# wi2 packed early into the vacated half of xT, low halves on VectorE, and each tile's maximum first: one edit to an attention + two-FFN kernel on Trainium2

## The chip, the cores and the metric

One core of one Trainium2 chip runs the whole program. The metric is device time in microseconds (us), the median of several executions. Engines: TensorE (PE for matmuls, PEld for weight loads), VectorE (DVE), ScalarE (ACT), GpSimd (POOL) and SyncE (SP, which here issues the loads).

## The reference

Three stages, all in float32:

```python
# attention: 2 batches x 8 heads, 576 tokens, head size 64, rotary q and k
attn = softmax(q_rot @ k_rot.T / 8);  x = attn @ v         # -> x: 1152 tokens x 512
# gated FFN, 512 -> 1536 -> 512
x2 = ((x @ w_a) * (x @ w_b)) @ w_out
# SoLU FFN, 512 -> 1024 -> 512
h = x2 @ w_in
solu = h * softmax(h)                                      # over the 1024 columns
ln = (solu - mean) / sqrt(var + 1e-6) * g_ln               # over the 1024 columns
out = ln @ w_out2
```

The FFN weights of this program arrive as 64-bit floats. The kernel reads them as pairs of 32-bit integers and puts float32 values together from them on the chip ("packing").

## The kernel before, in words

Every float32 matmul is done as three products of a high half and a low half (high x high, high x low, low x high). So each operand has two parts: the high half is a cast on ScalarE, the low half is the operand minus its high half, on VectorE or GpSimd.

**Weights.** 36 pieces of weights are numbered in the order of their use: 0 to 11 are w_a and w_b, 12 to 19 are w_out ("x", 768 columns each), 20 to 27 are wi2, the reference's second w_in ("h", 512 columns each), 28 to 35 are wo2 ("out", 512 columns each). For each piece, `load_n` allocates its place and lets SyncE issue the load into a raw buffer; `pack` builds float32 in a second buffer `f` in five steps (step 0 an absolute value on ScalarE, L87; steps 1 to 4 on VectorE, L89, L91, L93, L95); `split` makes the high half on ScalarE (`high`, L101, for "out" pieces behind a scaling, L100) and the low half (`low`, L104) on GpSimd, or on the engine that is passed. There are two raw and two `f` buffers, used in turn; from piece 20 on a buffer is two halves of 512 columns. `load_after(n)` issues the next loads once the last step of pack n stands in the queue, since the raw buffer is free from then on.

**Buffers that are used twice.** The three products of a, b and x are kept in `gT` tiles by token block t (0, 1, 2, of 384 tokens each). The split weights of wi2 go where `gT` of t = 0 was, those of wo2 where t = 1 was, and the rows `et` of the last stage where t = 2 was (the first one elsewhere). So wi2 can be split only when the last x2 block of t = 0 is done. `xT` (128 x 4 x 2 x 1152) holds x transposed, high and low, for the w_a/w_b matmuls (L580), and then x2 transposed.

**The x2 stage** (L705 to L729): 12 blocks (m, t) of 36 matmuls (L711), in the order (0,0) (0,1) (0,2) (1,0) (1,1) (1,2) (2,0) (3,0) (2,1) (3,1) (2,2) (3,2). Blocks with even m take turns in two PSUM buffers, those with odd m in two others. `x2_out` copies a block to `xT` on ScalarE (L718) and subtracts on VectorE (L719). Beside each block stand steps of the weights, by the dictionary `beside`.

**The last stage**, for nine tiles of 128 tokens: `hmm` (h, L744, 24 matmuls; two PSUM buffers in turn), `chain1` (the maximum on VectorE, L756; the exponential with its sum on ScalarE, L757), `chain2` (the sum's reciprocal, L762 and L763; the product that reads h in PSUM for the last time, L764; mean and variance, L767 to L770; a power on GpSimd, L772), `chain3` (L777), `ltp` (transposes on TensorE, L786; copy, L789; subtraction, L790), `out_half` (12 matmuls, L815) and `store`. h 0 to h 2 are mixed with the end of x2; from then on a loop runs h i+3, the first output half of tile i, `chain1` of i+3, `ltp` of i+1, the second output half of i, `chain2`, `store` and `chain3`.

The order on every engine is the order of the calls: nothing is rescheduled, and each engine works its queue in order. Waits follow from data and buffers.

Of the kernel before, what the change touches and what calls it, by code (L numbers as in the profile page):

```python
# [12 lines left out]
F32R = mybir.dt.float32r  # L13
I32 = mybir.dt.int32
AF = mybir.ActivationFunctionType
ALU = mybir.AluOpType
# [4 lines left out]
B, H, S, D = 2, 8, 576, 64  # L21
NT, DM, DF1, DF2 = B * S, 512, 1536, 1024
P = 128
NP = H // 2
# [4 lines left out]
CW = 384  # L29
# [40 lines left out]
def _raw(ap):  # L70
    return ap.bitcast(F32)
# [36 lines left out]
def attention_gated_ffn_solu_ffn(ctx: ExitStack, tc, q, k, v, wa, wb, wo1, wi2, wo2, gln, rope_cs, out):  # L108

    nc = tc.nc  # L110
    const = ctx.enter_context(tc.tile_pool(name="const", bufs=1))
# [6 lines left out]
    ident = const.tile([P, P], F32, name="ident")  # L118
    g_sb = const.tile([P, DF2 // P], F32, name="g_sb")
    mhalf = const.tile([P, 1], F32, name="mhalf")  # L120
    xT = const.tile([P, NP, 2, NT], F32R, name="xT")

# [2 lines left out]
    W, wt = {}, {}  # L127
# [7 lines left out]
    def load_w(key, w, raw, t):  # L135
        kind, n = key
        scale = None
        if kind == "ab":
            rv = raw.rearrange("p (m k c) t -> p m k (c t)", m=2, k=4)
            for m, src in enumerate((wa, wb)):  # L140
                nc.sync.dma_start(
                    out=rv[:, m], in_=src[:, 2 * n * P:2 * (n + 1) * P].rearrange("(k p) c -> p k c", p=P)
                )
        elif kind == "x":
            m, half = divmod(n, 2)
            raw, t = raw[:, :6 * P], t[:, :6 * P]
            nc.sync.dma_start(
                out=raw.rearrange("p (f c) t -> p f (c t)", f=6),
                in_=wo1[half * 6 * P:(half + 1) * 6 * P, 2 * m * P:2 * (m + 1) * P].rearrange("(f p) c -> p f c", p=P),
            )  # L150
        else:
            half = slice(n % 2 * DM, (n % 2 + 1) * DM)
            raw, t, w = raw[:, half], t[:, half], w[:, :, half]
            if kind == "h":
                src = wi2[n // 2 * P:(n // 2 + 1) * P, n % 2 * 2 * DM:(n % 2 + 1) * 2 * DM]
            else:
                src, scale = wo2[n * P:(n + 1) * P, :], g_sb[:, n:n + 1]
            nc.sync.dma_start(out=raw.rearrange("p c t -> p (c t)"), in_=src)
        W[key] = Weights(nc, raw, t, w, scale)
# [302 lines left out]

    def x_cols(u):
        b, pr = divmod(u, NP)
        return xT[:, pr, :, b * S:(b + 1) * S]

    def x_mult(u):
        if HI["x"] == "pool":
            nc.gpsimd.tensor_tensor(x_cols(u)[:, 0], x0[u], rb[u], op=ALU.mult)
        nc.gpsimd.tensor_tensor(x0[u], x0[u], rb.pop(u), op=ALU.mult)  # L470

    def x_hi(u):
        if HI["x"] != "pool":
            copy(HI["x"], x_cols(u)[:, 0], x0[u])

    def x_lo(u):
        dst = x_cols(u)
        nc.gpsimd.tensor_tensor(dst[:, 1], x0.pop(u), _raw(dst[:, 0]), op=ALU.subtract)
# [93 lines left out]
    gT, pab = {}, {}  # L572

    def ab_some(f, t, m, ks):
        if (f, t) not in pab:
            pab[f, t] = ps_s.tile([P, 2, 512], F32, tag="s", name=f"ab{f}_{t}")
        wf = W["ab", f].w.rearrange("p a (m k c) -> p a m k c", m=2, k=4)
        for kk in ks:
            for a, xa in ((0, 0), (0, 1), (1, 0)):
                nc.tensor.matmul(  # L580
                    pab[f, t][:, m, :CW], wf[:, a, m, kk, :], xT[:, kk, xa, t * CW:(t + 1) * CW],
                    start=(kk == a == xa == 0), stop=(kk == 3 and a == 1),
                )

# [15 lines left out]
    for f, loaded, steps in ((0, 54.0, W_POS[:6]), (1, W_POS[4] + 0.1, W_POS[6:])):  # L600
        key = ("ab", f)
        add(loaded, lambda key: load_w(key, wtile(w0, "w", key), raw0, f0), key)
        for i, pos in enumerate(steps[:5]):
            add(pos, lambda key, i: W[key].pack((i,)), key, i)
        for pos in steps[5:]:
            add(pos, lambda key: W[key].high(), key)
            add(pos + 1, lambda key: W[key].low(nc.gpsimd), key)
    for i, pos in enumerate(AB):
        add(pos, ab_some, 0, 0, i // 4, (i % 4,))
# [10 lines left out]
    NW, NX = len(order), NF + 8  # L620
    raw1, f1 = buffers(wp)

    def load_n(n):
        key = order[n]
        if n < NX:
            w = wtile((w0, wp)[n % 4 // 2], "w", key)
            odd = n % 2
        else:
            kind, half = key
            if half % 2 == 0:  # L630
                wt[kind, half // 2] = wtile(gpool, f"g{int(kind == 'out')}{half // 2}", key)
            w = wt[kind, half // 2]
            odd = half // 2 % 2
        load_w(key, w, *((raw1, f1), (raw0, f0))[odd])

    def load_after(n):

        ahead = (3,) if n == 1 else (n + 2,) if n < NX - 2 else (2 * n - NX + 4, 2 * n - NX + 5) if n < NX else (n + 4,)
        for m in ahead:
            if m < NW:  # L640
                load_n(m)

    def pack(n, steps=range(5)):
        W[order[n]].pack(steps)
        if 4 in steps:
            load_after(n)
# [24 lines left out]
    for i, (f, t) in enumerate(groups):  # L671
# [5 lines left out]
        for fn, *args in parts[ends[i - 1] if i else 0:ends[i]]:  # L677
            fn(*args)


    x2T = xT
    rest, dve = (1, 2, 3, 4), nc.vector
    beside = {
        (0, 0): [(pack, 15), (split, 15)],
        (0, 1): [(pack, 16)],
        (0, 2): [(pack, 17)],
        (1, 0): [(split, 16), (split, 17)],
        (1, 1): [(pack, 18)],
        (1, 2): [(pack, 19)],
        (2, 0): [(split, 18, dve), (split, 19, dve), (pack, 20), (pack, 21)],  # L690
        (3, 0): [(pack, 22), (pack, 23)],
        (2, 1): [
            (split, 20, dve), (split, 21), (pack, 24, (0,)), (split, 22), (pack, 24, rest), (pack, 25, (0,)), (split, 23),
            (pack, 25, rest),
        ],
        (3, 1): [
            (pack, 26), (split, 24), (pack, 27), (split, 25), (pack, 28, (0,)), (pack, 29, (0,)),
            (pack, 28, rest),
        ],
        (2, 2): [  # L700
            (split, 26), (split, 27), (pack, 29, rest), (pack, 30), (pack, 31, (0,)), (split, 28), (split, 29), (pack, 31, rest),
        ],
    }

    def x2_mm(m, t):  # L705
        pool, tag = ((ps_t, "t"), (ps_o, "o"))[m % 2]
        px[m, t] = o = pool.tile([P, 512], F32, tag=tag, name=f"x2_{m}_{t}")
        for f in range(NF):
            wx = W["x", 2 * m + f // 6].w[:, :, f % 6 * P:(f % 6 + 1) * P]
            for a, ga in ((0, 0), (0, 1), (1, 0)):  # L710
                nc.tensor.matmul(  # L711
                    o[:, :CW], wx[:, a], gT[f // 3, t][:, f % 3, ga], start=(f == 0 and a == ga),
                    stop=(f == NF - 1 and a == 1),
                )

    def x2_out(m, t):
        o, c0 = px.pop((m, t)), t * CW
        nc.scalar.copy(x2T[:, m, 0, c0:c0 + CW], o[:, :CW])  # L718
        nc.vector.tensor_tensor(  # L719
            x2T[:, m, 1, c0:c0 + CW], o[:, :CW], _raw(x2T[:, m, 0, c0:c0 + CW]), op=ALU.subtract  # L720
        )

    px = {}
    order_x2 = [(m, t) for m in (0, 1) for t in range(3)] + [(m, t) for t in range(3) for m in (2, 3)]
    for m, t in order_x2[:-2]:
        x2_mm(m, t)
        for fn, *args in beside[m, t]:
            fn(*args)
        x2_out(m, t)  # L729


    NK2 = DF2 // P
# [3 lines left out]
    def hmm(i):  # L736
        s = ps_s.tile([P, 2, 512], F32, tag="s", name=f"h{i}")
        ph[i] = s
        c0 = i * P
        idx = 0  # L740
        for kk in range(4):
            for xa, a in ((0, 0), (0, 1), (1, 0)):
                for c in range(2):
                    nc.tensor.matmul(  # L744
                        s[:, c], x2T[:, kk, xa, c0:c0 + P], wt["h", kk][:, a, c * 512:(c + 1) * 512],
                        start=(idx == 0), stop=(idx == 11),
                    )
                idx += 1
# [76 lines left out]

    for fn, *args in (
        (x2_mm, 2, 2), *beside[2, 2], (hmm, 0), (x2_out, 2, 2),
        (x2_mm, 3, 2), (pack, 32, (0,)), (split, 30), (chain1, 0), (pack, 33, (0,)), (pack, 32, rest), (split, 31),  # L830
        (chain2, 0), (hmm, 1), (x2_out, 3, 2), (pack, 34, (0,)), (chain3, 0), (pack, 33, rest), (split, 32),
        (chain1, 1), (hmm, 2), (pack, 35, (0,)), (pack, 34, rest), (split, 33), (chain2, 1), (ltp, 0), (split, 34),
        (chain3, 1), (pack, 35, rest), (chain1, 2), (split, 35), (chain2, 2), (chain3, 2),
    ):
        fn(*args)
    for i in range(NTT):
        j = i + 3
        if j < NTT:
# [49 lines left out]
```

## Time and profile before

| what | value |
|---|---|
| median of 3 runs (lowest to highest) | 521.57 us (521.37 to 522.39) |
| the profiled execution, its own time | 522.98 us |
| its span, first to last instruction | 520.1 us |
| mean granted TensorE clock over the span | 0.984 of full speed |
| busy: PE / PEld / DVE / ACT / POOL | 492.8 / 463.7 / 383.9 / 270.0 / 178.3 us |

Times in rows are counted from the start of the span. A row of a time line gives the start, the busy time, the engine, the source line, the operation and what it writes and reads; in brackets stands how long the engine was idle before it and who released it. x followed by a number counts instructions merged into the row. The granted clock is given as a share of full speed (2.4 GHz).

### The profile page before, as it was taken

To read this page: it belongs to the slowest core of one execution; us is meant where nothing else is said; L and a number is where in the kernel's file an instruction comes from. 1 tells how busy PE (TensorE), PEld (TensorE's weight loads), DVE (VectorE), ACT (ScalarE), POOL (GpSimd) and SP (SyncE) were. 2 spreads that over 40 slices of the span, in tenths; PEclk is the share of its full clock that TensorE was granted. 3 is DMA by queue.
4 is the path that set the end of the run, shared out by engine and by line. 5 is a ranking of instruction groups with operands and counts; after the bars stand their busy time and mean duration, and the time that the engine had idled before them with its cause. 6 is when DMAs were issued, how large, how long until landed. Compare 5 with 4: busy or idle time off the path is not lost.

```text
span 520.1 us, 7992 instructions
## 1 busy us (share of the span) xinstructions
PE 492.8 (95%) x2992; PEld 463.7 (89%) x2992; DVE 383.9 (74%) x595; ACT 270.0 (52%) x562; POOL 178.3 (34%) x128
## 2 busy tenths in 40 slices
PE   4889999999989999999999999999999969999997
PEld 4779988989888999999999999999999848888886
DVE  5899999999999767666756755645899996755450
ACT  2699998998898444343444333332354433222221
POOL 5598988788135003111122311220054321000000
PEclk9699999999999999999999999999999979999999
DMA  5334223225002143222332111334434200000011
GB/s 142 85 94 104 70 72 95 73 70 153 25 13 93 45 151 129 82 81 82 102 110 93 62 62 60 122 121 136 172 101 161 81 0 21 20 22 20 21 40 40
DMA packets 50914, 41.97 MB, mean 81 GB/s; under 512 B 23765, under 2 KB 46868, under 8 KB 50876
## 3 DMA queue, kind: packets, MB, share of 16 engines
q1 hardware_dynamic: 50124, 40.48, 26.0%
q10 hardware_dynamic: 624, 0.82, 0.5%
q8 instruction: 23, 0.38, 0.3%
q0 software_dynamic: 128, 0.17, 0.2%
q14 instruction: 15, 0.12, 0.1%
HBM read 37.00 MB, written 2.39 MB: 76 GB/s over the span
## 4 chain that ended last, share of the span: by engine, by line
PE 69%; DVE 15%; ACT 7%; DMA 4%; issue 2%; SPq 1%; POOL 1%; POOLq 0%; DVEq 0%; ACTq 0%
PE ab L580 29%; PE x L711 10%; PE out L815 10%; PE h L744 7%; PE pv L405 4%; PE s L327 4%; ACT e L344 2%; PE t L356 2%; DVE f L95 2%; DVE f L93 2%; DMA qd<-in_q_dram 2%; DVE nm L336 2%; DVE f L91 1%; PE lt L786 1%; ACT pT L370 1%
## 5 line engine op out<-in xcount | busy, mean ns | idle before, releaser
L580 PE MATMUL ab<-xT,wab 128*128 128x384 f32 x864 | 151.9, 336 | 0.0
L580 PEld LDWEIGHTS ab<-xT,wab 128*128 128x128 f32 x864 | 150.7, 188 | 0.1
L711 PE MATMUL x<-gT,wx 128*128 128x384 f32 x432 | 75.9, 336 | 0.0
L711 PEld LDWEIGHTS x<-gT,wx 128*128 128x128 f32 x432 | 75.6, 188 | 0.1
L104 POOL TENSOR_TENSOR wab<-f,wab 128x1024 fp32r<-128x1024 f32 x11 | 26.4, 2398 | 119.2 <-ACT wab L101 103.2
L327 PE MATMUL s<-kS,qS 128*128 128x288 f32 x320 | 60.1, 316 | 1.2 <-ACT e L344 1.2
L744 PE MATMUL h<-wh,xT 128*128 128x512 f32 x216 | 54.4, 409 | 5.1 <-DVE et L764 5.1
L344 ACT ACTIVATE e<-s,nm 128x576 f32<-128x576 f32 x72 | 53.5, 743 | 5.7 <-DVE nm L336 5.0
L744 PEld LDWEIGHTS h<-wh,xT 128*128 128x128 f32 x216 | 42.4, 197 | 15.5 <-issue 5.0
L336 DVE TENSOR_REDUCE nm<-s 128x1 f32<-128x576 f32 x72 | 53.7, 746 | 2.2 <-PE s L327 1.2
L815 PE MATMUL out<-wout,lnT 128*128 128x512 f32 (+1 forms) x240 | 52.9, 373 | 0.0
L374 DVE TENSOR_TENSOR pT<-t,pT 128x512 fp32r<-128x512 f32 x72 | 49.4, 686 | 3.2 <-ACT pT L370 2.2
L327 PEld LDWEIGHTS s<-kS,qS 128*128 128x128 f32 x320 | 47.2, 195 | 4.2 <-ACT e L344 3.4
L815 PEld LDWEIGHTS out<-wout,lnT 128*128 128x128 f32 x240 | 41.4, 188 | 7.5
L405 PE MATMUL pv<-pT,V 128*128 128x288 f32 x288 | 46.0, 304 | 0.8 <-DVE pT L392 0.5
L356 PE MATMUL t<-ident,e 128*128 128x128 f32 x288 | 43.9, 275 | 0.1
L370 ACT CAST pT<-t 128x512 fp32r<-128x512 f32 x72 | 42.3, 587 | 1.1 <-PE t L356 0.5
L405 PEld LDWEIGHTS pv<-pT,V 128*128 128x128 f32 x288 | 39.3, 188 | 2.0 <-POOL V L251 0.8
L588 ACT COPY a<-ab 128x384 f32<-128x384 f32 x36 | 17.3, 479 | 45.4 <-PE ab L580 44.7
L597 DVE TENSOR_TENSOR gT<-a,gT 128x384 fp32r<-128x384 f32 x36 | 23.1, 641 | 21.8 <-ACT gT L596 21.8
L89 DVE TENSOR_SCALAR f<-f 128x512 f32<-128x512 f32 (+2 forms) x36 | 28.7, 797 | 12.5 <-ACT f L87 12.5
L757 ACT ACTIVATE et<-h,mx 128x1024 f32<-128x1024 f32 x9 | 10.0, 1116 | 52.1 <-DVE mx L756 52.1
(132 smaller groups left out, 712.2 us busy)
## 6 DMA issues: line engine op xcount, KB each, us to landing
raw<-in_moe_w_a_dram SPq DMA_DIRECT2D x12, 512.0 KB
raw<-in_moe_w_b_dram SPq DMA_DIRECT2D x12, 512.0 KB
raw<-in_moe_w_out_dram SPq DMA_DIRECT2D x8, 768.0 KB
raw<-in_moe_w_in_dram SPq DMA_DIRECT2D x8, 512.0 KB
raw<-in_moe_w_out_dram SPq DMA_DIRECT2D x8, 512.0 KB
kraw<-in_k_dram SPq DMA_DIRECT2D x16, 128.0 KB
vraw<-in_v_dram SPq DMA_DIRECT2D x8, 256.0 KB
qd<-qd SPq DMA_DIRECT2D x7, 288.0 KB
```

Of the source, the lines that this page charges most:

```text
L89: eng.tensor_scalar(_raw(t), _raw(t), LOW_END, HIGH_END, op0=ALU.max, op1=ALU.min)
L327: nc.tensor.matmul(s[:, c, :KC], qS[u % 2][:, a, off:off + P], kS[u % 2][:, h, c * KC:(c + 1) * KC], start=(m == 0), stop=(m == last),)
L336: nc.vector.tensor_reduce(t, ps[n][:, :, :KC], axis=AX.XY, op=ALU.max, negate=True)
L344: nc.scalar.activation(t.rearrange("p (c n) -> p c n", c=2), ps.pop(n)[:, :, :KC], AF.Exp, bias=nm.pop(n), accum_out=sums[u][:, i:i + 1],)
L356: nc.tensor.transpose(t[:, j, :], e[n][:, j * P:(j + 1) * P], ident)
L370: nc.scalar.copy(hi, src)
L374: nc.vector.tensor_tensor(lo, src, _raw(hi), op=ALU.subtract)
L405: nc.tensor.matmul(o[:, :KC], w[:, h, 4 if m == 8 else m % 4].rearrange("p a d -> p (a d)"), t[:, m, c * KC:(c + 1) * KC], start=(m == 0), ...
L580: nc.tensor.matmul(pab[f, t][:, m, :CW], wf[:, a, m, kk, :], xT[:, kk, xa, t * CW:(t + 1) * CW], start=(kk == a == xa == 0), stop=(kk == 3 ...
L711: nc.tensor.matmul(o[:, :CW], wx[:, a], gT[f // 3, t][:, f % 3, ga], start=(f == 0 and a == ga), stop=(f == NF - 1 and a == 1),)
L744: nc.tensor.matmul(s[:, c], x2T[:, kk, xa, c0:c0 + P], wt["h", kk][:, a, c * 512:(c + 1) * 512], start=(idx == 0), stop=(idx == 11),)
L815: nc.tensor.matmul(o[:, cols], t[:, la, kk, :], w[:, a, cols], start=(kk == la == a == 0), stop=(kk == NK2 - 1 and la == 1),)
```

## The change

- `xT` becomes four tiles, one for each m. The tiles of m = 2 and 3, which x2 needs late, are given up after the w_a/w_b stage: two staging tiles take their place, and pieces 20 to 27 are packed there and not in `f`. x2 of m = 2 and 3 is allocated there again when its first block is written (in `x2_out`), once the staged pieces are split.
- The loads follow a new table: pieces 20 to 23 are loaded behind packs 16 and 17, ahead of 18 and 19.
- Packs 20 to 23 move into blocks (1,0) and (1,1), pack 18 into (1,2), pack 19 into (2,0), packs 24 to 27 into (2,0) and (3,0). Splits 20 to 27 stand together in block (2,1), ahead of the outputs of (2,0) and (3,0).
- All low halves from piece 15 on are made on VectorE.
- In the last list, `chain1` of a tile stands ahead of steps of the packs, and these stand between `chain1` and `chain2`.

```diff
@@ -118,7 +118,8 @@
-    xT = const.tile([P, NP, 2, NT], F32R, name="xT")
+    xp = ctx.enter_context(tc.tile_pool(name="xp", bufs=1))
+    xT = [xp.tile([P, 2, NT], F32R, tag=f"x{m}", name=f"xT{m}") for m in range(NP)]
@@ -152,6 +153,7 @@
             if kind == "h":
+                t = staged[n // 4][:, n % 4]
                 src = wi2[n // 2 * P:(n // 2 + 1) * P, n % 2 * 2 * DM:(n % 2 + 1) * 2 * DM]
...
@@ -633,10 +635,11 @@
+    waiting = {1: (3,), 16: (20, 21), 17: (22, 23), 20: (), 21: (18,), 22: (), 23: (19,), 18: (24, 25), 19: (26, 27)}
+
     def load_after(n):
-
-        ahead = (3,) if n == 1 else (n + 2,) if n < NX - 2 else (2 * n - NX + 4, 2 * n - NX + 5) if n < NX else (n + 4,)
-        for m in ahead:
+        for m in waiting.get(n, (n + 2 if n < 16 else n + 4,)):
             if m < NW:
                 load_n(m)
@@ -678,29 +681,11 @@
-    x2T = xT
+    x2T = list(xT)
+    staged = [xp.tile([P, 4, DM], I32, tag=f"x{m}", name=f"staged{m}") for m in (2, 3)]
     rest, dve = (1, 2, 3, 4), nc.vector
-    beside = {
-        (0, 0): [(pack, 15), (split, 15)],
-        (0, 1): [(pack, 16)],
-        (0, 2): [(pack, 17)],
-        (1, 0): [(split, 16), (split, 17)],
-        (1, 1): [(pack, 18)],
-        (1, 2): [(pack, 19)],
-        (2, 0): [(split, 18, dve), (split, 19, dve), (pack, 20), (pack, 21)],
-        (3, 0): [(pack, 22), (pack, 23)],
-        (2, 1): [
-            (split, 20, dve), (split, 21), (pack, 24, (0,)), (split, 22), (pack, 24, rest), (pack, 25, (0,)), (split, 23),
-            (pack, 25, rest),
-        ],
...
     def x2_out(m, t):
+        if m > 1 and t == 0:
+            x2T[m] = xp.tile([P, 2, NT], F32R, tag=f"x{m}", name=f"x2T{m}")
         o, c0 = px.pop((m, t)), t * CW
-        nc.scalar.copy(x2T[:, m, 0, c0:c0 + CW], o[:, :CW])
+        nc.scalar.copy(x2T[m][:, 0, c0:c0 + CW], o[:, :CW])
...
-    for m, t in order_x2[:-2]:
-        x2_mm(m, t)
-        for fn, *args in beside[m, t]:
-            fn(*args)
-        x2_out(m, t)
+    run(
+        (x2_mm, 0, 0), (pack, 15), (split, 15, dve), (x2_out, 0, 0),
+        (x2_mm, 0, 1), (pack, 16), (x2_out, 0, 1),
+        (x2_mm, 0, 2), (pack, 17), (x2_out, 0, 2),
+        (x2_mm, 1, 0), (split, 16, dve), (split, 17, dve), (pack, 20), (pack, 21), (x2_out, 1, 0),
+        (x2_mm, 1, 1), (pack, 22), (pack, 23), (x2_out, 1, 1),
+        (x2_mm, 1, 2), (pack, 18), (x2_out, 1, 2),
+        (x2_mm, 2, 0), (split, 18, dve), (pack, 19), (split, 19, dve), (pack, 24),
+        (x2_mm, 3, 0), (pack, 25), (pack, 26), (pack, 27),
+        (x2_mm, 2, 1), (split, 20, dve), (split, 21, dve), (split, 22, dve), (split, 23, dve), (x2_out, 2, 0),
+        (split, 24, dve), (split, 25, dve), (split, 26, dve), (split, 27, dve), (x2_out, 3, 0),
+        (x2_out, 2, 1),
+        (x2_mm, 3, 1), (pack, 28), (pack, 29), (pack, 30), (x2_out, 3, 1),
+    )
@@ -825,14 +824,14 @@
-    for fn, *args in (
-        (x2_mm, 2, 2), *beside[2, 2], (hmm, 0), (x2_out, 2, 2),
-        (x2_mm, 3, 2), (pack, 32, (0,)), (split, 30), (chain1, 0), (pack, 33, (0,)), (pack, 32, rest), (split, 31),
-        (chain2, 0), (hmm, 1), (x2_out, 3, 2), (pack, 34, (0,)), (chain3, 0), (pack, 33, rest), (split, 32),
-        (chain1, 1), (hmm, 2), (pack, 35, (0,)), (pack, 34, rest), (split, 33), (chain2, 1), (ltp, 0), (split, 34),
-        (chain3, 1), (pack, 35, rest), (chain1, 2), (split, 35), (chain2, 2), (chain3, 2),
-    ):
-        fn(*args)
+    run(
+        (x2_mm, 2, 2), (split, 28, dve), (split, 29, dve), (pack, 31), (pack, 32, (0,)), (split, 30, dve), (hmm, 0),
+        (x2_out, 2, 2), (split, 31, dve), (pack, 32, (1, 2)), (x2_mm, 3, 2), (pack, 33, (0,)), (chain1, 0),
+        (pack, 32, (3, 4)), (chain2, 0), (hmm, 1), (pack, 34, (0,)), (chain3, 0), (pack, 33, rest), (split, 32, dve),
+        (x2_out, 3, 2), (pack, 35, (0,)), (chain1, 1), (hmm, 2), (pack, 34, rest), (split, 33, dve), (chain2, 1),
+        (ltp, 0), (chain3, 1), (split, 34, dve), (pack, 35, (1, 2)), (chain1, 2), (pack, 35, (3, 4)), (chain2, 2),
+        (split, 35, dve), (chain3, 2),
+    )
```

The matmuls index `xT[m]` and `x2T[m]` in place of `xT[:, m]`; `run` calls a list of steps in order.

## Rows read from the trace of the kernel before

**Rows 1.** Busy time by stretch; columns as in the first line.

```profile
core 0: us, PE busy (x) PEld busy (x) DVE busy (x) ACT busy (x) POOL busy (x), PEclk, DMA share, GB/s
324.40:362.80 38.40, 38.40 (x221) 38.40 (x220) 21.40 (x28) 11.03 (x18) 7.36 (x4) 1.00 0.36 118
...
393.65:423.00 29.35, 24.27 (x117) 20.52 (x117) 28.13 (x43) 14.62 (x26) 8.90 (x8) 0.98 0.28 88
423.01:431.33 8.32, 8.32 (x25) 6.62 (x26) 7.25 (x12) 2.15 (x4) 2.24 (x3) 0.67 0.00 0
437.76:443.35 5.59, 5.59 (x26) 4.53 (x25) 3.74 (x8) 2.65 (x5) 0.00 (x0) 1.00 0.13 47
```

**Rows 2.** Time line of TensorE: h 1, h 2 and h 3.

```profile
405.50 5.74 PE L744 MATMUL h<-wh,xT 128*128 128x512 f32 x24
411.58 5.81 PE L744 MATMUL h<-wh,xT 128*128 128x512 f32 x24 [0.34 <-DVE et L764]
...
423.01 8.32 PE L744 MATMUL h<-wh,xT 128*128 128x512 f32 x24 [4.75 <-DVE et L764]
```

**Rows 3.** The chain that ended last: start, time, what (an output half, the transposes).

```profile
431.33 2.78 PE out L815 x12
434.11 0.87 PE lt L786 x8
```

**Rows 4.** Time line of all engines: a low half on GpSimd and a pack's step.

```profile
385.92 1.29 POOL L104 TENSOR_TENSOR wh<-f,wh 128x512 fp32r<-128x512 f32 x1 [1.28 <-PE x L711]
386.02 1.48 DVE L91 TENSOR_SCALAR f<-f 128x512 int32<-128x512 int32 x1
```

**Rows 5.** Groups by line, VectorE, 376.4 to 431 us: count, busy, mean ns, idle before.

```profile
L95 DVE SCALAR_TENSOR_TENSOR f<-raw,f 128x512 int32<-128x512 int32 x12 | 11.4, 951 | 0.4
L93 DVE SCALAR_TENSOR_TENSOR f<-raw,f 128x512 int32<-128x512 int32 x12 | 11.3, 941 | 0.4
```

**Rows 6.** The same view, VectorE, 364 to 376.4 us, GpSimd idle.

```profile
L93 DVE SCALAR_TENSOR_TENSOR f<-raw,f 128x512 int32<-128x512 int32 x4 | 2.8, 692 | 0.1
...
L104 DVE TENSOR_TENSOR wh<-f,wh 128x512 fp32r<-128x512 f32 x1 | 0.7, 692 | 0.0
```

**Rows 7.** Time line of VectorE: lows 18 and 19, pack 20, later a subtraction and maximum 0.

```profile
363.62 1.83 DVE L104 TENSOR_TENSOR wx<-f,wx 128x768 fp32r<-128x768 f32 x2 [0.23 <-ACT wx L101]
365.37 0.42 DVE L89 TENSOR_SCALAR f<-f 128x512 f32<-128x512 f32 x1
...
367.01 0.69 DVE L95 SCALAR_TENSOR_TENSOR f<-raw,f 128x512 int32<-128x512 int32 x1
367.62 0.42 DVE L89 TENSOR_SCALAR f<-f 128x512 f32<-128x512 f32 x1
...
405.85 0.55 DVE L719 TENSOR_TENSOR xT<-x,xT 128x384 fp32r<-128x384 f32 x1
406.32 1.21 DVE L756 TENSOR_REDUCE mx<-h 128x1 f32<-128x1024 f32 x1
```

**Rows 8.** Time lines of SyncE's queue and ScalarE: a 512 KB load, and its first reader.

```profile
385.25 0.33 SPq L158 DMA_DIRECT2D raw<-in_moe_w_out_dram  x1
...
388.77 0.68 ACT L87 ACTIVATE f<-raw 128x512 f32<-128x512 f32 x1 [2.35 <-DMA raw<-in_moe_w_out_dram]
```

**Rows 9.** Groups by line, ScalarE, 393.65 to 431 us.

```profile
L100 ACT ACTIVATE f<-f,g_sb 128x512 f32<-128x512 f32 x7 | 5.0, 717 | 2.4 <-DVE f L95 2.4
L101 ACT CAST wout<-f 128x512 fp32r<-128x512 f32 x7 | 4.3, 620 | 0.2
L757 ACT ACTIVATE et<-h,mx 128x1024 f32<-128x1024 f32 x3 | 3.3, 1116 | 16.0 <-DVE mx L756 16.0
...
L757 ACT ACTIVATION_READ_ACCUMULATOR et<-h,mx 128x1 f32 x2 | 0.4, 193 | 0.0
```

**Rows 10.** Time line of VectorE in a later tile: `chain2` and `chain3`.

```profile
449.79 0.15 DVE L762 TENSOR_SCALAR sm<-sm 128x1 f32<-128x1 f32 x1
...
450.17 1.28 DVE L764 SCALAR_TENSOR_TENSOR et<-et,sm,h 128x1024 f32<-128x1024 f32 x1
...
453.93 0.81 DVE L777 TENSOR_SCALAR et<-et,mv,rs 128x1024 f32<-128x1024 f32 x1 [0.73 <-POOL rs L772]
```

More of the change, by code (lines that the diff above doesn't have):

```diff
@@ L464, in x_cols @@
         b, pr = divmod(u, NP)
-        return xT[:, pr, :, b * S:(b + 1) * S]
+        return xT[pr][:, :, b * S:(b + 1) * S]
     def x_mult(u):
@@ L580, in ab_some @@
                 nc.tensor.matmul(
-                    pab[f, t][:, m, :CW], wf[:, a, m, kk, :], xT[:, kk, xa, t * CW:(t + 1) * CW],
+                    pab[f, t][:, m, :CW], wf[:, a, m, kk, :], xT[kk][:, xa, t * CW:(t + 1) * CW],
                     start=(kk == a == xa == 0), stop=(kk == 3 and a == 1),
@@ L678, in attention_gated_ffn_solu_ffn @@
             fn(*args)
-    x2T = xT
+    x2T = list(xT)
+    staged = [xp.tile([P, 4, DM], I32, tag=f"x{m}", name=f"staged{m}") for m in (2, 3)]
     rest, dve = (1, 2, 3, 4), nc.vector
-    beside = {
-        (0, 0): [(pack, 15), (split, 15)],
-        (0, 1): [(pack, 16)],
-        (0, 2): [(pack, 17)],
-        (1, 0): [(split, 16), (split, 17)],
-        (1, 1): [(pack, 18)],
-        (1, 2): [(pack, 19)],
-        (2, 0): [(split, 18, dve), (split, 19, dve), (pack, 20), (pack, 21)],
-        (3, 0): [(pack, 22), (pack, 23)],
-        (2, 1): [
-            (split, 20, dve), (split, 21), (pack, 24, (0,)), (split, 22), (pack, 24, rest), (pack, 25, (0,)), (split, 23),
-            (pack, 25, rest),
-        ],
[L696 to L703, printed above, removed]
     def x2_mm(m, t):
@@ L716, in x2_out, with run @@
     def x2_out(m, t):
+        if m > 1 and t == 0:
+            x2T[m] = xp.tile([P, 2, NT], F32R, tag=f"x{m}", name=f"x2T{m}")
         o, c0 = px.pop((m, t)), t * CW
-        nc.scalar.copy(x2T[:, m, 0, c0:c0 + CW], o[:, :CW])
+        nc.scalar.copy(x2T[m][:, 0, c0:c0 + CW], o[:, :CW])
         nc.vector.tensor_tensor(
-            x2T[:, m, 1, c0:c0 + CW], o[:, :CW], _raw(x2T[:, m, 0, c0:c0 + CW]), op=ALU.subtract
+            x2T[m][:, 1, c0:c0 + CW], o[:, :CW], _raw(x2T[m][:, 0, c0:c0 + CW]), op=ALU.subtract
         )
+    def run(*steps):
+        for fn, *args in steps:
+            fn(*args)
     px = {}
-    order_x2 = [(m, t) for m in (0, 1) for t in range(3)] + [(m, t) for t in range(3) for m in (2, 3)]
-    for m, t in order_x2[:-2]:
-        x2_mm(m, t)
-        for fn, *args in beside[m, t]:
-            fn(*args)
-        x2_out(m, t)
+    run(
[12 more added lines that the diff above has]
+    )
     NK2 = DF2 // P
@@ L744, in hmm @@
                     nc.tensor.matmul(
-                        s[:, c], x2T[:, kk, xa, c0:c0 + P], wt["h", kk][:, a, c * 512:(c + 1) * 512],
+                        s[:, c], x2T[kk][:, xa, c0:c0 + P], wt["h", kk][:, a, c * 512:(c + 1) * 512],
                         start=(idx == 0), stop=(idx == 11),
```

## The prediction

> **What bounds the kernel now.** I read the stretches by busy time first, then TensorE's order of work, then the rows of the engine that releases it. From 324.40 to 362.80 us TensorE is busy without a break and VectorE only 21.40 of 38.40 us; from 393.65 to 423.00 it is the other way round: VectorE 28.13 of 29.35 us, TensorE 24.27 [rows 1]. So near the end of the x2 stage the bound passes to VectorE for about 30 us. What that costs stands in TensorE's order of work: the scores matmul of tile 2 (h, L744) begins at 411.58 after a wait, that of tile 3 at 423.01 after 4.75 us, both for line 764 of VectorE (the product in `chain2`, the last reader of the PSUM buffer) [rows 2]. Tile 3's own matmul then takes 8.32 us at a granted clock of 0.67 of full speed, against 5.59 us for the same work at 1.00 [rows 1]. The mean of 0.67 is part 1.2, part 2.4 GHz; TensorE had sat idle just ahead of it, so I let these 2.73 us go with the wait.
>
> **What is to be had.** From the start of h 1 at 405.50 [rows 2], which nothing delays, TensorE has this to do until h 4: h 1, h 2, h 3 at 5.59 each [rows 1], two output halves at 2.78 and two transposes lt at 0.87 [rows 3]: 16.77 + 5.56 + 1.74 = 24.07 us, so h 4 could begin at 429.57. It began at 437.76 [rows 1]. The difference, **8.19 us**, is 5.46 us of waits and 2.73 us of clock, and is the most the change can bring; after it VectorE is no longer the bound (3.74 busy of 5.59 us [rows 1]).
>
> **Low halves from GpSimd to VectorE.** Before, 15 low halves of the 512-wide weights (21 to 35) run on GpSimd. While one of them runs, a VectorE instruction on SBUF data stands: L104 on GpSimd from 385.92 to 387.21, and L91 from 386.02 takes 1.48 us and ends 0.29 us behind it [rows 4]. The two long steps of a pack (L93, L95) average 941 and 951 ns over the 12 packs beside GpSimd [rows 5], but 692 ns where GpSimd was idle [rows 6]: 12 x (0.249 + 0.259) = 6.1 us, and the short steps are stretched too. On VectorE such a low half takes 0.69 us [rows 6], and as its last 0.08 us lie under the next instruction (L95 at 367.01, the next at 367.62 [rows 7]) the queue moves by 0.61: 15 x 0.61 = 9.2 us added for over 6.1 returned. This part alone loses up to 3 us on VectorE or roughly breaks even. SBUF — State Buffer of the Trainium skill, Who interferes with whom, calls the pair of ports that the two engines share an exclusive lock for a whole instruction: by that, 15 x 1.29 = 19.4 us would come back, VectorE would have time to spare everywhere below, and the sum would be the whole 8.19 us; the averages bear out less.
>
> **wi2 packed early.** A pack moves the queue by 2.25 us (365.37 to 367.62 [rows 7]). Packs 20 to 23, 9.0 us, go from behind 362 to between 345 and 356, where VectorE had 17 of 38 us free and ScalarE, which does their first step, 27 [rows 1]; lows 15 to 17 (2.8 us) come there too. Pack 19 goes the other way (768 columns, at most 1.5 times 2.25, 3.4). Cover: TensorE runs x2 there and waits only for weights 15 to 19. Without it (VectorE full) 5.6 us would be back in the tight stretch. New targets in xT's vacated half also free packs 24 to 27 from waiting for split 20 to 23. The split of xT into four tiles changes no instruction: nothing. Loads: 20 to 23 are issued behind packs 16 and 17 in blocks (0,1) and (0,2) and read a block or two later; 18 and 19 now stand behind packs 21 and 23 on SyncE's queue. A 512 KB load is read 3.5 us after its issue (385.25 to 388.77 [rows 8]), 768 KB at 1.5 times that, 5.3. Load 18, issued near 351, is wanted at 356.3 and has 3 us more before split 18 can start at all; load 19, issued near 356, is wanted at 363.3. Nothing queued behind them is late for its reader.
>
> **The walk on VectorE.** It decides, so I follow it with these steps. TensorE needs 36 x 0.174 = 6.3 us for one x2 block (38.40 us for 221 matmuls [rows 1]). Low 18 begins at 363.62 as before, 0.92 us [rows 7]: 364.5. Pack 19: 367.9. Its high half on ScalarE, at most 0.93 (1.5 x 0.62 [rows 9]), then low 19: 369.7; block (3,0) reads it halfway, about 371.6: 1.9 us to spare. Packs 24 to 27: 378.7. Lows 20 to 23, 2.4: 381.2. Here is the added wait: x2's (2,0) may be written only when they have left the staging tile; ScalarE's copy (under 0.62) holds up high 24 to 27 queued behind it, and VectorE waits for the copy, then subtracts (0.47, 405.85 to 406.32 [rows 7]): 382.3. Block (2,2) wants that PSUM buffer at 387.5. Lows 24 to 27, copy, two subtractions: 386.4; h 0 needs them at 393.65. Packs 28 to 30, a subtraction, lows 28 and 29: 394.9. Pack 31: 397.1. Low 30 and a subtraction: 398.2; then 0.3 us until ScalarE has scaled and copied weight 31 (0.72 + 0.62 [rows 9]); low 31: 399.1. **The maxima first:** tile 0's maximum (1.21 [rows 7]) goes between steps of pack 32, whose last two hide the exponential (1.12 + 0.19 [rows 9]): 402.6. h 0 has ended by then (393.65 + 5.59); before, the maximum began only at 406.32 [rows 7]. `chain2` and `chain3` take 4.95 (449.79 to 454.74 in an undisturbed tile [rows 10]): 407.6. Pack 33, low 32, last subtraction: 410.9. h 1 ends at 411.09, so VectorE is there in time, by 0.2 us. Then maximum 1 to 412.3, exponential to 413.6, scaling and copy of weight 33 to 414.95 (pack 34 lies beside these), low 33 to 415.6, and line 764 ends 1.66 us later [rows 10]: 417.2. TensorE is through h 2 and lt 0 at 411.09 + 5.59 + 0.87 = 417.55. h 3 finds its buffer free, 0.35 us ahead.
>
> What is late next: low 35, now behind `chain2` of tile 2. From 417.2: statistics 1.75 (451.45 to 453.20 [rows 10]), two subtractions for lt at the price of a low (1.3), L777 0.81 [rows 10], low 34 0.6, pack 35 2.25, maximum 2 1.2, `chain2` 3.4, low 35 0.7: 429.2. The last quarter of tile 0's output matmul wants it at 417.55 + 5.59 + 2.78 + 0.87 + 2.09 = 428.9. Stall 0.3.
>
> **Sum.** 8.19 - 0.3 = 7.9 us. The profiled execution took 522.98 us (span 520.10), 1.41 over the median of the runs; 515.1 in its own time, **513.7** against the median. Less than 0.2% (1.04 us) could not be told from no change.
>
> **Rivals.** *(a) VectorE still late at h 3.* The two margins make 0.55 us in a queue of 47 us with some fifteen hand-overs to ScalarE that I price at nothing extra. For it: 1.5% more is enough, and each further us is a us of stall. Against: 768-wide steps and copies are taken at upper bounds. A stall of 2 us gives 515.7; if the clock falls again as behind the 4.75 us wait (it did not behind 0.34 [rows 2]), up to 518.5.
> *(b) Slower: the stretched rows are not GpSimd's doing.* Then 9.2 us are added to a full VectorE and nothing returns. Packs 24 to 35 stay at 941 and 951 ns, line 764 of tile 1 ends at 417.2 + 6.1 - 0.2 = 423.1 by the long steps alone, and at 427.1 if four of the 24 short steps are 1 us longer, as L91 was. h 3 began at 423.01 before: wait and clock loss stay, and 4.1 us come on top, 525.7. It decides from 5.9 us of stretch left over. Against it: without GpSimd no long step was long [rows 6]. Perfetto Trace Analysis of the Trainium skill, Optimizing Scalar/DVE Operations, holds that with VectorE saturated some work may be better off on ScalarE or even GpSimd, which speaks against this change, and adds that the shared port may undo it; by the first half 525.7 comes out, and the trace bears out the second.
> *(c) The early packs do not come early* (staging tiles or loads held back). Then 5.6 us stay in the tight stretch, line 764 ends at 422.6, and wait and clock loss stay: 521.5, no change. For it: all loads share one queue in a new order. Against: x2, which reads xT no more, has been running since 324.4 [rows 1], 20 us by then.
>
> **Numbers.** The forecast 0.72, (a) 0.20, (b) 0.04, (c) 0.04. Faster by over 0.2%: the forecast and nearly all of (a) and a little of (c), 0.93; within: 0.03; slower: 0.04. Low end: all 8.19 and 0.3 of spread, 513.1. High end: 517.0, which takes in (a) up to 3.3 us; beyond lie its clock loss, (b) and (c).
>
> **What would show it.** Right: h 3 without a wait and at full clock, near 417.6; L93 and L95 at about 692 ns throughout; packs 20 to 23 before 357; maximum 1 right at the end of h 1. Wrong: a wait of h 3 on line 764 (a); long L93 and L95 with GpSimd idle (b); packs 20 to 23 behind 362, or any x2 matmul that waits (c); a wait of over 0.5 us for low 35.

## The result, and the profile after

The changed kernel takes **515.11 us** (median of 4 runs, 514.62 to 515.76) against 521.98 us (4 runs) before: ratio 0.9869, 95% interval 0.985 to 0.9888, 6.9 us less. A second comparison of the unaltered kernel gave 514.9 against 522.49 us: 0.9859 (0.9838 to 0.9879), 7.6 us less. The prediction was 513.7 us in a range of 513.1 to 517.0, and 7.9 us less.

The busy time of the changed kernel by stretch, cut at the places that answer to [rows 1] (columns as there):

```profile
324.88:363.30 38.42, 38.42 (x221) 38.42 (x221) 28.84 (x43) 12.53 (x21) 1.84 (x1) 1.00 0.45 143
363.30:394.16 30.86, 30.86 (x178) 30.86 (x177) 27.77 (x48) 15.85 (x28) 0.00 (x0) 1.00 0.50 164
394.16:417.96 23.80, 23.80 (x118) 20.59 (x117) 20.86 (x38) 10.85 (x19) 0.56 (x1) 1.00 0.15 45
417.96:423.60 5.64, 5.64 (x27) 4.60 (x25) 5.54 (x11) 2.15 (x4) 0.55 (x1) 1.00 0.00 0
430.05:435.63 5.58, 5.58 (x25) 4.52 (x24) 3.76 (x7) 2.65 (x5) 0.00 (x0) 1.00 0.08 28
```

TensorE is busy for the whole of every stretch shown, and its granted clock is 1.00 (2.4 GHz) in each. VectorE does 28.84 us in the first, where it did 21.40. GpSimd has one low half of an earlier piece left in the first stretch (1.84 us), and behind it nothing but the powers of `chain2` (0.55 us each).

TensorE's time line from h 1 to h 4, which answers to [rows 2]. h now stands in two rows, since two of its inputs keep the name xT and two are called x2T:

```profile
406.01 2.94 PE L743 MATMUL h<-wh,xT 128*128 128x512 f32 x12
408.79 2.95 PE L743 MATMUL h<-wh,x2T 128*128 128x512 f32 x12
411.58 2.95 PE L743 MATMUL h<-wh,xT 128*128 128x512 f32 x12
414.37 2.95 PE L743 MATMUL h<-wh,x2T 128*128 128x512 f32 x12
417.16 1.03 PE L785 MATMUL lt<-ident,et 128*128 128x128 f32 x8
417.96 3.02 PE L743 MATMUL h<-wh,xT 128*128 128x512 f32 x12
...
427.19 3.03 PE L814 MATMUL out<-wout,lnT 128*128 128x512 f32 x12
430.05 2.95 PE L743 MATMUL h<-wh,xT 128*128 128x512 f32 x12
```

No row has a wait in brackets. From the start of h 1 to the start of h 4 it is 430.05 - 406.01 = **24.04 us**. The prediction had put the floor of this stretch at 24.07. In the kernel before it was 32.10, from 405.50 [rows 2] to this row, the start of h 4:

```profile
437.60 5.75 PE L744 MATMUL h<-wh,xT 128*128 128x512 f32 x24
```

The prediction had h 4 begin at 437.76 [rows 1]; that is the end of the output half before it (434.74 + 3.03 in the time line). Rows of the time line overlap by some 0.16 us, so only starts may be compared with starts. The distance from start to start is used below as the yardstick for every kernel, because it leaves out where a run's x2 stage happens to begin (from 324.0 to 326.0 us over all profiles of this study). It comes from one profiled execution of each kernel.

VectorE's groups by line from 364 to 431 us answer to [rows 5, 6]:

```profile
L95 DVE SCALAR_TENSOR_TENSOR f<-raw,f 128x512 int32<-128x512 int32 x8 | 5.5, 692 | 0.3
L93 DVE SCALAR_TENSOR_TENSOR f<-raw,f 128x512 int32<-128x512 int32 x8 | 5.5, 689 | 0.2
L104 DVE TENSOR_TENSOR wout<-f,wout 128x512 fp32r<-128x512 f32 x8 | 5.4, 686 | 0.7 <-ACT wout L101 0.7
L104 DVE TENSOR_TENSOR wh<-staged,wh 128x512 fp32r<-128x512 f32 x8 | 5.0, 686 | 0.0
```

The long steps of a pack are down from 941 and 951 ns to 689 and 692, and a low half costs 686.

And this is how VectorE's queue runs where it decides, in the time line (last `x2_out`, maximum 1, low 33, line 764, which is now 763):

```profile
410.27 0.55 DVE L706 TENSOR_TENSOR x2T<-x,x2T 128x384 fp32r<-128x384 f32 x1
411.78 1.22 DVE L755 TENSOR_REDUCE mx<-h 128x1 f32<-128x1024 f32 x1 [0.95 <-PE h L743]
...
415.54 0.69 DVE L104 TENSOR_TENSOR wout<-f,wout 128x512 fp32r<-128x512 f32 x1 [0.28 <-ACT wout L101]
...
416.53 1.28 DVE L763 SCALAR_TENSOR_TENSOR et<-et,sm,h 128x1024 f32<-128x1024 f32 x1
```

VectorE now waits 0.95 us for h 1, and line 763 ends at 417.81, just ahead of h 3.

### The profile page after: what moved, and what is told of

Its sections match the earlier page's. It is cut to its first block, busy times and chain, and to the rows that moved or that the text cites. A ratio compares the mean times of both kernels' runs of the same rounds, so it can differ in the third digit from the quotient of the medians.

```text
span 512.8 us, 7967 instructions
## 1 busy us (share of the span) xinstructions
PE 490.0 (96%) x2992; PEld 461.8 (90%) x2992; DVE 384.2 (75%) x613; ACT 270.2 (53%) x562; POOL 152.8 (30%) x110
## 4 chain that ended last, share of the span: by engine, by line
PE 82%; DVE 9%; ACT 5%; issue 2%; DMA 1%; POOL 0%; DVEq 0%; ACTq 0%; POOLq 0%
PE ab L582 29%; PE x L696 15%; PE h L743 10%; PE out L814 10%; PE pv L407 6%; PE s L329 5%; PE t L358 3%; ACT e L346 3%; DVE nm L338 2%; PE lt L785 2%; DVE pT L376 1%; DMA qd<-in_q_dram 1%; DVE V L235 1%; DVE x L421 1%; ACT pT L372 1%
## 5 line engine op out<-in xcount | busy, mean ns | idle before, releaser
L771 POOL TENSOR_TENSOR rs<-mv,mhalf 128x1 f32<-128x1 f32 x9 | 5.3, 585 | 156.6 <-DVE mv L769 156.6
L598 ACT CAST gT<-a 128x384 fp32r<-128x384 f32 x36 | 18.5, 513 | 34.9 <-DVE a L591 34.9
L591 DVE TENSOR_TENSOR a<-ab,a 128x384 f32<-128x384 f32 x36 | 20.0, 554 | 21.2 <-ACT a L590 20.9
L358 PEld LDWEIGHTS t<-ident,e 128*128 128x128 f32 x288 | 34.9, 141 | 0.7 <-DVE pT L376 0.3
```

The costliest lines, as they stand in the source:

```text
L358: nc.tensor.transpose(t[:, j, :], e[n][:, j * P:(j + 1) * P], ident)
```

## The experiments

The yardstick of each kernel and what h 3 did. Each ratio is against the kernel before in the same comparison. "Waited" is the figure in brackets of the time line, and "took" runs from the start of h 3 to the start of the output half behind it. The edits of the first two are shown against the kernel before, all others against the changed kernel.

| kernel | ratio to before (95%) | h 1 to h 4 | h 3 waited | h 3 took |
|---|---|---|---|---|
| before | 1 | 32.10 | 4.75 | 8.16 |
| before, again | 1.0004 (0.9988 to 1.0019) | 32.32 | 4.75 | 8.39 |
| four tiles for xT alone | 1.0003 (0.9992 to 1.0014) | 31.51 | 4.74 | 7.59 |
| lows alone | 0.999 (0.9975 to 1.0004) | 30.18 | 4.37 | 7.16 |
| early packs alone | 0.9899 (0.988 to 0.9918) | 26.21 | 1.92 | 5.65 |
| changed, packs late | 0.9979 (0.9964 to 0.9994) | 30.58 | 3.68 | 8.26 |
| changed, lows back on GpSimd | 0.9926 (0.9907 to 0.9945) | 28.01 | 2.60 | 5.65 |
| changed, old list | 0.9916 (0.9901 to 0.9931) | 25.63 | 1.08 | 5.65 |
| changed, three lows more | 0.9885 (0.987 to 0.99) | 25.73 | 1.44 | 5.65 |
| changed, seven lows more | 0.998 (0.9967 to 0.9992) | 30.89 | 4.34 | 7.92 |
| changed | 0.9869 (0.985 to 0.9888) | 24.04 | none | 5.65 |
| changed, again | 0.9859 (0.9838 to 0.9879) | 24.05 | none | 5.65 |

**Four tiles for xT alone.** The first question was whether the other layout costs something, as x2 began 0.51 us later than before in the first profile.

```diff
-    xT = const.tile([P, NP, 2, NT], F32R, name="xT")
+    xT = [xp.tile([P, 2, NT], F32R, tag=f"x{m}", name=f"xT{m}") for m in range(NP)]
...
```

> The kernel before with nothing but xT as four tiles. In the changed kernel's profile x2 begins at 324.88 us, before at 324.37, and the last instructions end 0.3 us later behind the last matmul; my theory is that this half microsecond is start-up and spread and not the change: no difference, within 0.2%, with h 3 waiting near 4.75 us as before. Rival: the new layout of xT costs it, +0.5 to +0.8 us in every run, x2 beginning near 324.9.

522.19 against 522.16 us: no difference that can be measured. Nor does x2 begin late by the change: in a second profile of the kernel before it began at 324.85, against 324.88 in the changed kernel.

**Lows alone.** The order of before, no early packs.

```diff
-        (0, 0): [(pack, 15), (split, 15)],
+        (0, 0): [(pack, 15), (split, 15, dve)],
...
```

> The kernel before, in its own order, with all low halves from piece 15 on VectorE and nothing packed early. My theory (GpSimd's lows hold VectorE up by about 11 us in the tight stretch, and 9.2 us of lows take their place): L93 and L95 fall to 0.69 us, about 2 us are gained at most, h 3 still waits some 3 to 4.5 us for line 764: -0.5 to -2 us. Rival, the stretch is not GpSimd's doing: L93 and L95 stay at 0.94 us and the time is 4 to 9 us longer. Rival, the lows are all that matters: h 3 does not wait and the time is that of the changed kernel, -7 us.

521.67 against 522.16 us, and the interval reaches 1.0004, so this part alone is worth nothing that is clear of the measurement. But the long steps fell as far as in the changed kernel (VectorE's groups by line, 364 to 431 us):

```profile
L93 DVE SCALAR_TENSOR_TENSOR f<-raw,f 128x512 int32<-128x512 int32 x16 | 11.1, 693 | 0.6
L95 DVE SCALAR_TENSOR_TENSOR f<-raw,f 128x512 int32<-128x512 int32 x16 | 11.1, 692 | 0.5
...
L104 DVE TENSOR_TENSOR wout<-f,wout 128x512 fp32r<-128x512 f32 x7 | 4.7, 685 | 1.7 <-ACT wout L101 1.7
```

This refutes rival (b): the stretch was GpSimd's doing. It is also what the prediction said of this part, that what VectorE gets back it spends on the lows. On top of it VectorE waits 1.7 us for ScalarE's high halves, which GpSimd used to wait for.

**Early packs alone.** Staging, early packs and the new loads; lows on GpSimd and the last list as before.

```diff
...
-        (x2_mm, 1, 0), (split, 16, dve), (split, 17, dve), (pack, 20), (pack, 21), (x2_out, 1, 0),
+        (x2_mm, 1, 0), (split, 16), (split, 17), (pack, 20), (pack, 21), (x2_out, 1, 0),
...
```

> Of the change only the staging tiles, the early packs and the loads: lows 15 to 17 and 21 to 35 on GpSimd, the last list in the order of before. Early packs take 5.9 us out of the tight stretch and the holding-up by GpSimd stays. My theory: the early packs are the larger half (late packs cost the changed kernel 5.6 us, lows on GpSimd 2.7): h 3 waits 0 to 3 us at full clock, 3.5 to 7 us faster than before. Rival, the parts need one another (a full queue, any one missing brings the wait and the clock loss back): no more than 2 us faster than before.

516.73 against 522.11 us, 5.4 less. This is the largest single part, and it carries most of the gain. TensorE still waits, but behind 1.92 us the granted clock is 1.00:

```profile
420.14 3.03 PE L743 MATMUL h<-wh,xT 128*128 128x512 f32 x12 [1.92 <-DVE et L763]
```

VectorE's part in this is smaller (by the yardstick the gain is 5.9 us). h 3 began 14.10 us after h 1, and 17.51 before: 3.4 us earlier. Another 2.5 us is the clock (h 3 took 5.65 in place of 8.16). What kept VectorE from more is a wait that the prediction does not have. The low halves 20 to 27 now stand together in one block, and here they are on GpSimd: ScalarE's copy of x2 waits for GpSimd, and VectorE's subtraction for the copy (time lines of ScalarE and VectorE):

```profile
388.98 0.86 ACT L705 CAST x2T<-x 128x384 fp32r<-128x384 f32 x2 [3.58 <-POOL wh L104]
389.50 1.02 DVE L706 TENSOR_TENSOR x2T<-x,x2T 128x384 fp32r<-128x384 f32 x2 [5.59 <-ACT x2T L705]
```

In the changed kernel, with these low halves on VectorE, the same subtraction waits a tenth of that:

```profile
385.54 1.02 DVE L706 TENSOR_TENSOR x2T<-x,x2T 128x384 fp32r<-128x384 f32 x2 [0.55 <-ACT x2T L705]
```

**Changed, packs late.** The opposite: only the place of packs 18 to 23 and the loads go back.

```diff
...
-        (x2_mm, 1, 1), (pack, 22), (pack, 23), (x2_out, 1, 1),
-        (x2_mm, 1, 2), (pack, 18), (x2_out, 1, 2),
+        (x2_mm, 1, 1), (pack, 18), (x2_out, 1, 1),
+        (x2_mm, 1, 2), (pack, 19), (x2_out, 1, 2),
...
```

> The changed kernel with packs 20 to 23 back in blocks (2,0) and (3,0), packs 18 and 19 in (1,1) and (1,2), and the loads in the order of before; lows stay on VectorE, staging stays. 9.0 us come back into the tight stretch and pack 19's 3.1 leave it: VectorE is 5.9 us later, of which it had 0.95 us of slack ahead of maximum 1 and about 0.2 behind it. My theory: h 3 waits 3.5 to 4.8 us, and with the clock's loss behind such a wait (2.7 us) the time is 4 to 7.5 us above the changed kernel, close to the kernel before. Rival, where the packs stand does not matter (the lows did it): as the changed kernel.

520.74 us, 5.6 above the changed kernel. h 3 in TensorE's time line:

```profile
423.03 5.46 PE L743 MATMUL h<-wh,xT 128*128 128x512 f32 x12 [3.68 <-DVE et L763]
428.28 3.17 PE L743 MATMUL h<-wh,x2T 128*128 128x512 f32 x12
431.29 2.96 PE L814 MATMUL out<-wout,lnT 128*128 128x512 f32 x12
```

Wait 3.68 us, and 8.26 us for h 3 in place of 5.65. The 5.9 us of VectorE time that come back, less about 1.1 of slack, would make 4.8; the wait was within the expectation, at its lower end. From h 1 to h 3 it is 15.86 us against 11.95, 3.9 us more, and h 3 itself takes 2.6 us more.

**Changed, lows back on GpSimd.**

```diff
...
-        (x2_mm, 2, 2), (split, 28, dve), (split, 29, dve), (pack, 31), (pack, 32, (0,)), (split, 30, dve), (hmm, 0),
+        (x2_mm, 2, 2), (split, 28), (split, 29), (pack, 31), (pack, 32, (0,)), (split, 30), (hmm, 0),
...
```

> The changed kernel with the low halves 15 to 17 and 21 to 35 back on GpSimd; early packs and the new order stay. My theory: 15 lows of 0.61 us leave VectorE (9.2) and 11 us of holding up come back, so line 763 of tile 1 is some 1 to 3 us later, h 3 waits 0.5 to 3 us and low 35 comes late: 1 to 4 us slower than the changed kernel, L93 and L95 near 0.9 us again. Rival, an exclusive lock for the whole instruction: 15 x 1.29 = 19.4 us come back, h 3 waits over 7 us, slower than the kernel before. Rival, GpSimd's help is worth its price: as the changed kernel.

517.85 us, 2.7 above the changed kernel. TensorE's waits from 320 us on, and VectorE's two long steps (364 to 431 us):

```profile
PE h L743 <- DVE et L763: 2.6, 1, 2.6
PE out L814 <- POOL wout L104: 0.9, 1, 0.9
```

```profile
L95 DVE SCALAR_TENSOR_TENSOR f<-raw,f 128x512 int32<-128x512 int32 x8 | 8.7, 1082 | 0.3
...
L93 DVE SCALAR_TENSOR_TENSOR staged<-raw,staged 128x512 int32<-128x512 int32 x4 | 3.7, 935 | 0.1
L95 DVE SCALAR_TENSOR_TENSOR staged<-raw,staged 128x512 int32<-128x512 int32 x4 | 3.7, 934 | 0.1
```

The steps are long again where GpSimd works. The second wait is a queue effect: low 35 now stands on GpSimd behind the power of tile 2, and the output matmul waits 0.9 us for it. The rule in SBUF — State Buffer of the Trainium skill, Who interferes with whom, that the shared pair of ports is locked for the whole instruction, was taken in the prediction and in my rival for all that VectorE does: 15 x 1.29 us, and here a wait of over 7. The wait was 2.60. The same section exempts VectorE instructions with at most one input from SBUF, outside modes that use both pairs of ports, and the trace agrees with that: line 763, whose second large input is h in PSUM, ran beside a low half on GpSimd and took 1.28 us as it does alone.

```profile
418.48 1.28 DVE L763 SCALAR_TENSOR_TENSOR et<-et,sm,h 128x1024 f32<-128x1024 f32 x1
418.51 1.28 POOL L104 TENSOR_TENSOR wout<-f,wout 128x512 fp32r<-128x512 f32 x1 [6.98 <-ACT wout L101]
```

In sum VectorE's steps from 364 to 431 us took 8.0 us more than in the changed kernel, and its subtractions behind ScalarE's copies of x2 waited 6.2 us in place of 1.1. That makes some 13 us, against 9.2 us of low halves that left it. h 3 began 2.8 us later after h 1, and the 0.95 us that maximum 1 waits for h 1 in the changed kernel took up most of the rest.

**Changed, old list.** Lows on VectorE and early packs stay; the last list has the order of before.

```diff
...
-        (x2_out, 2, 2), (split, 31, dve), (pack, 32, (1, 2)), (x2_mm, 3, 2), (pack, 33, (0,)), (chain1, 0),
-        (pack, 32, (3, 4)), (chain2, 0), ...
+        (x2_mm, 3, 2), (pack, 32, (0,)), (split, 30, dve), (chain1, 0), (pack, 33, (0,)), (pack, 32, rest), (split, 31, dve),
+        (chain2, 0), ...
```

> The changed kernel with the order of before in the last list (chain1 and the steps of packs 32 to 35); early packs, staging and lows on VectorE stay, and pack 31 stays behind splits 28 and 29. In the old list maximum 0 already stood ahead of pack 32 and maximum 1 ahead of pack 34; only maximum 2 moves. My theory: the maxima were late before because VectorE's queue was, not by their place, so the list is worth little: h 3 waits at most 1 us, h 4 some 0.5 us: 0 to +2 us on the changed kernel. Rival, as the prediction had it, the order of the maxima carries a good part: +3 us or more.

517.85 us, 2.7 above the changed kernel: more than my theory allowed, less than the rival. What the list does shows in VectorE's time line (maximum 0, lows 33 and 35), with one row of ScalarE's in between:

```profile
400.41 1.22 DVE L755 TENSOR_REDUCE mx<-h 128x1 f32<-128x1024 f32 x1 [1.62 <-PE h L743]
...
415.37 0.66 ACT L87 ACTIVATE f<-raw 128x512 f32<-128x512 f32 x1
...
417.32 0.69 DVE L104 TENSOR_TENSOR wout<-f,wout 128x512 fp32r<-128x512 f32 x1 [0.85 <-ACT wout L101]
...
429.78 0.69 DVE L104 TENSOR_TENSOR wout<-f,wout 128x512 fp32r<-128x512 f32 x1 [2.53 <-ACT wout L101]
```

A low half waits until ScalarE is through the exponential, the scaling and the high half. Low 35 stands right behind its maximum in the old list and waits 2.53 us with VectorE idle; in the changed kernel it stands behind `chain2` and does not wait. Low 33 has the steps of pack 34 ahead of it in both lists. What differs is ScalarE's queue: in the old list the absolute value of piece 35 (at 415.37) stands between the exponential and the scaling, in the changed kernel ahead of both, and the wait is 0.85 against 0.28 us. Maximum 0 stands too early in the old list: it waits 1.62 us for h 0, where the changed kernel puts low 31 and two steps of pack 32 first and has no wait. So the list pays through what stands between the steps that wait for another engine, not through the maxima being early: maximum 0 stands later than in the old list, maximum 1 follows low 32 in both, and only maximum 2 moves forward. By the yardstick this is 1.6 of the 2.7 us. About 1.0 us falls behind h 4 (83.8 us from there to the end, against 82.8), where TensorE's only wait is 0.29 us for ScalarE; the rest is open.

**Three and seven lows more.** Low 32 computed again on VectorE, right behind maximum 1.

```diff
-        (x2_out, 3, 2), (pack, 35, (0,)), (chain1, 1), (hmm, 2), (pack, 34, rest), (split, 33, dve), (chain2, 1),
+        (x2_out, 3, 2), (pack, 35, (0,)), (chain1, 1), *[(low, 32, dve)] * 3, (hmm, 2), (pack, 34, rest), (split, 33, dve), (chain2, 1),
```

> The changed kernel with low 32 computed three times more on VectorE, right behind maximum 1: 3 x 0.61 = 1.83 us added where the walk leaves 0.2 us. My theory: h 3 waits 1.4 to 1.8 us for line 763 and runs at full clock as it did behind 2.60 us: +1.4 to +1.9 us on the changed kernel. Rival, there is more room than the walk says: no wait, no difference. Rival, any wait there costs clock: +3 us or more.

> As the kernel with three more, with seven: 7 x 0.61 = 4.27 us added. My theory: h 3 waits 3.9 to 4.3 us, and behind such a wait (3.68 us with late packs, 4.37 to 4.75 elsewhere) the clock falls: h 3 takes 7.3 to 8.3 in place of 5.6 us: +5.6 to +7 us on the changed kernel, about the kernel before. Rival, the clock's loss belongs to something else that the change removed: +4.1 us.

With three, 516.17 us: 1.1 above the changed kernel by the medians (1.3 against its second run), 1.7 by the yardstick, where I expected 1.4 to 1.9. With seven, 520.87 us: 5.8 above, 6.9 by the yardstick. The busy time of h 3 in the two kernels, three first:

```profile
419.39:425.04 5.65, 5.65 (x25) 4.59 (x25) 5.55 (x11) 0.50 (x1) 0.55 (x1) 1.00 0.00 0
```

```profile
421.95:429.87 7.92, 7.92 (x24) 6.29 (x25) 7.71 (x16) 1.71 (x3) 0.55 (x1) 0.69 0.00 0
```

The first waited 1.44 us and kept 1.00; the second waited 4.34 and ran at 0.69, a mean of the 1.2 and the 2.4 GHz level. The added lows moved VectorE's queue by more than the 0.61 us each of my expectation: three by 2.05 us (412.67 to 414.72), seven by 4.96 (412.33 to 417.29). From h 1 to h 3 it is 13.63 and 16.53 us against 11.95, so h 3 came 1.68 and 4.58 us later. Both say that the margin at h 3 is 0.4 us; beyond it the kernel is on VectorE again.

**Both kernels again.** No edit.

> The changed kernel, unaltered, for a tighter ratio and a second profile. The first profile held the whole 8.2 us between the start of x2 and the start of h 4, yet the median fell by 6.9. My theory: the waits are gone in every run, and the difference is the clock term (2.73 us in the profile I worked from, 1.73 to 2.67 in other profiles with such a wait) and 1 us of spread at the start; then 514.5 to 515.5, 6.7 to 7.5 us under the kernel before. Rival: the full 8.2 us is there and the first four runs were slow ones: 513.9 or less.

> The kernel before, unaltered, for a second profile of it. My theory: h 3 again waits 4.4 to 4.8 us, and its clock loss is another than 2.73 us (h 3 takes 7.3 to 8.3 us in place of 5.59), x2 begins within 1 us of 324.4. Rival: the clock loss is 2.7 us each time, and the prediction's sum was too large for another reason.

514.9 us is where I expected it, but not for my reason. I had taken the clock's loss in the first profile for a large one. The row of h 3 is 8.55 us in the second profile of the kernel before, more than the 7.3 to 8.3 that I expected and more than the 8.32 of the first:

```profile
412.04 5.81 PE L744 MATMUL h<-wh,xT 128*128 128x512 f32 x24 [0.32 <-DVE et L764]
...
423.47 8.55 PE L744 MATMUL h<-wh,xT 128*128 128x512 f32 x24 [4.75 <-DVE et L764]
```

Over the three profiles of before's order of work (twice before, once with four tiles) h 3 took 2.5, 2.7 and 1.9 us more than 5.65, 2.4 on the mean. From the start of x2 to the end of the span before took 195.7 (520.1 - 324.37) and 195.9 us (520.8 - 324.85), the changed kernel 187.9 both times (512.8 - 324.88, 513.0 - 325.06): 7.8 to 8.0 us less. The first comparison's interval reaches from 5.8 to 7.8 us and the second's from 6.3 to 8.5, so the medians' 6.9 and 7.6 us do not contradict that; nothing in the runs asks for another cause.

## Why the prediction was right

**The bound and the floor.** Right. TensorE's order of work needs 24.07 us by the rows of before and took 24.04. What was to be had is 8.03 us by starts (32.10 - 24.07), not 8.19, and the clock's part of it is 2.5 us (8.16 against 5.65), not 2.73: the prediction measured once from a start and once from an end. The changed kernel is 8.06 us under the one before by this yardstick, and 8.27 in the second pair of profiles.

**The walk on VectorE.** Right nearly to the tenth where it decides. With x2 begun 0.51 us later, the walk has line 764 of tile 1 ending at 417.7 and h 1 ending at 411.6; the trace has 417.81 and VectorE released by h 1 at 411.78. Ahead of maximum 1 its upper bounds made it 0.6 us late: the last subtraction ended at 410.82, the walk had 411.4. That did no harm because VectorE then waits for h 1 in either case.

**Low halves from GpSimd to VectorE.** Right: no gain by itself (0.999, interval up to 1.0004). The price for GpSimd's hold from the averages was nearer than the 19.4 us by the lock alone: VectorE's steps from 364 to 431 us took 11 us more in the kernel before than with lows alone. What the prediction did not have is that beside the early packs these low halves are worth more than their own time, since on GpSimd they hold up x2's copies.

**wi2 packed early.** Right in kind; that the size agrees is luck. 5.6 us of VectorE's time were to leave the tight stretch, and the early packs alone brought 5.4 us, their removal cost 5.6. But in these two h 3 came only 3.4 us earlier and 3.9 us later after h 1; the clock made 2.5 and 2.6 us of the difference. Without the low halves on VectorE part of what the early packs gave was lost again in the 5.59 us wait behind GpSimd.

**The maxima first.** The step that failed. The prediction gave this part no price of its own and took maximum 0's late start [rows 7] as a matter of its place. The order of before had it earlier still, ahead of the steps of pack 32; it was late because the queue was. What the list brought, 2.7 us, is mostly cover for waits on other engines: without it the low halves on VectorE wait for high halves, and maximum 0 for h 0. The walk had this cover in its times, but I did not see that it was the list's doing.

**What is late next.** I had 0.3 us of stall for low 35. There was none: it ended at 429.30, just when the last quarter of the output matmul came to it, and h 4 began at 430.05.

**The parts together.** The prediction priced each by its own VectorE time. Their worths do not add up: lows alone 0.5 us, early packs alone 5.4, all 6.9 to 7.6; and early packs with one of the other two were no better than without (0.9926 and 0.9916 against 0.9899). Low halves on GpSimd hold up x2's copies (5.59 us in both kernels that have them there beside early packs), and there the new list puts low 35 behind a power. Low halves on VectorE bring waits for ScalarE, and the list covers them. So only both together are worth more than neither. The list without early packs was not run.

**The rivals.** (a) did not come about, but it was near: 0.4 us of margin, and 2.05 us more work made it real. (b) fell with the lows alone, (c) with the place of packs 20 to 23, which end at 356.7 on VectorE.

## What to carry to other kernels

When two engines take turns at being the bound, look for a stretch where the late one is idle and buffer space has already been given up, and move work there: here it gave 5.4 us by itself, and moving the low halves to the other engine gave nothing clear. An operation moved to the busier engine brings its waits for other engines into that engine's queue, so move it together with independent work that fills them. Changes of this kind have to be measured together as well as one by one: a wait that one of them brings can hide what another gives. Judge such a change by the time between two landmarks of the bounding engine, which here separated 24.04 from 25.73 us where the intervals of the two ratios overlap (up to 0.9888, and from 0.987).

## What the runs showed of the hardware that was not expected

The clock's loss is not proportional to the wait. Behind waits of 1.08, 1.44, 1.92 and 2.60 us h 3 ran at 1.00 and took 5.65 us; behind 3.68, 4.34, 4.37 and 4.74 to 4.75 us it always lost, but (against 5.65) 2.6, 2.3, 1.5 and 1.9 to 2.7 us, the most behind one of the longest and nearly as much behind the shortest of them. Each is one profiled execution. So rival (a) was cheaper than its upper end said for waits up to 2.6 us: it would have cost the wait alone.
